# Linear attention and mixture-of-depths on one core: the early loads, one copy, one exponential and the warm-up rearranged

## Chip, cores and metric

One core of a Trainium2 chip runs the whole program. The metric is the device time of one execution in microseconds (us). Three runs of the kernel before took 196.46, 196.93 and 198.37 us; the median is 196.93 us.

## What is computed

The program is an attention block without a softmax over pairs, followed by a block that sends 128 of 576 rows of each batch through a small MLP. There are 8 batches, 8 heads, 576 rows and 64 columns per head.

```python
q_s = exp(q - max(q, -1));  q_s /= sum(q_s, -1)
k_s = exp(k - max(k, 2));   k_s /= sum(k_s, 2)
kv  = einsum('bhsd,bhse->bhde', k_s, v)
x   = einsum('bhsd,bhde->bhse', q_s, kv)     # regrouped to (8, 576, 512)
scores = x @ w_gate
out = x
for b: top = the 128 rows of b with the highest score
       xe = x[b, top]
       out[b, top] = xe + sigmoid(scores[b, top]) * (relu(xe @ w1) @ w2)
```

w1 is 512 x 1024 and w2 is 1024 x 512, all in float32.

## The kernel before

A *unit* is a batch and half of its heads, so there are 16 units u = 0 to 15, two per batch. The raw inputs of a unit are loaded into tiles `raw["q"]`, `raw["k"]`, `raw["v"]`; there are three of each (`LD = 3`), so the load of unit u + 3 waits until unit u is read. Every load is cut into two DMAs, all issued by SyncE's queue (SP) except one half of k(0), which ScalarE issues. A DMA that is issued takes the next of eight completion semaphores in turn, and waits for the DMA that had it eight issues earlier.

For one unit, ScalarE takes the exponential of k (`k_exp`, tile ke) and of q (`q_exp`, tile qe, two parts of 5 and 4 row groups). An engine copies v into a tile `v_ones` with columns of ones beside it (`v_copy`, or `v_copy_part` by half of the heads). TensorE (PE) multiplies ke with v_ones (`kv_mm`, or `kv_mm_parts` for unit 1), VectorE (DVE) normalizes that into `kv_w` (`kv_out`, `kv_out_part`), PE transposes qe (`q_t`), ScalarE or VectorE copies the result out of PSUM to qT, and PE multiplies qT with kv_w (`x_mm`). VectorE takes sums and scales (`x_sums`, `x_scale`), and SP stores the rows (`x_store`).

When both units of a batch are done, the scores are known (`score`). PE and ScalarE lay them out as a row (`score_row`, tile srow), and VectorE compares each row group with it (`compare`, line 443) to get a rank. For batch 0 alone, `select` (lines 498 to 512) turns the ranks into a 0/1 matrix and PE multiplies the rows with it, so that the chosen rows are gathered and transposed at once: five rounds of compare, one-hot matrix and matmuls. The other batches fetch their rows by an indirect DMA. The MLP runs on PE in pieces between the attention steps.

Nothing is scheduled by a planner here: `manual_schedule` keeps every engine to the order of the code, and lines 857 to 930 write out by hand the order of units 0 to 2, which is where the change lies. Before that, 12 matmuls on ones (line 173, `WARM = 12`) keep PE busy from the start. The lines that the change and the prediction speak of are: 220 to 223 (the memsets of the unused last row group of k(1), v(1), k(2), and the loads of unit 1 and of k(2)), 871 to 876 (the memset of v(2) by VectorE between the two halves of `q_t(0)`, then the loads of v(2), q(2) and of w1), 885 and 886 (v(1) copied half by VectorE and half by GpSimd), and 906 to 913 (score, `kv_mm(2)` in two halves around `score_row(0)`, and the exponentials of q(2)).

Of the kernel before, what the change touches and what calls it, by code (L numbers as in the profile page):

```python
# [17 lines left out]
def kernel(  # L18
# [23 lines left out]
    nc = tc.nc  # L42
    B, H, S, D = q.shape
    DM, F = moe_w1.shape
    P = 128
    R = 5
    N2 = R - 1
# [13 lines left out]
    NV = 5  # L61
    TURNED = frozenset((11, 13, 15))
    HC = 32
    WARM = 12
    assert S == 64 * T and D == 64 and DM == H * D and DM == 512 and H % 4 == 0
    assert 1 < capacity < S and KF == 8 and NQ == 2
    assert B * S <= 32 * 256
# [31 lines left out]
    def rows_of(b, upward):  # L99
# [12 lines left out]
    def load(u, which, queues=(nc.sync, nc.sync)):  # L112
        b, qd = units[u]
        for what in which:
            src = {"q": q, "k": k, "v": v}[what]
            t = raw[what][u % LD]
            first = src[place(b), 4 * qd].offset
            if what == "q" and u in by_vector:

                for g in range(4):  # L120
                    i, c = divmod(g, 2)
                    nc.sync.dma_start(
                        out=t.rearrange("p h r d -> p (h r d)")[HC * g:HC * (g + 1)],
                        in_=bass.AP(tensor=src.tensor, offset=first + 2 * i * SD + HC * c,
                                    ap=[[T * D, HC], [D, T], [SD // 2, 4], [1, HC]]))
                continue
            if what == "q":
                for h in range(2):
                    queues[h].dma_start(out=t[:, h].rearrange("p r d -> p (r d)"),
                                        in_=bass.AP(tensor=src.tensor, offset=first + 2 * h * SD,  # L130
                                                    ap=[[T * D, P], [1, T * D]]))
                continue
            for n, rows in ((1, N2), (0, R)):
                queues[n].dma_start(
                    out=t[n::2, :, :rows].rearrange("p h r d -> p h (r d)"),
                    in_=bass.AP(tensor=src.tensor, offset=first + n * R * D,
                                ap=[[T * D, 64], [SD, 4], [1, rows * D]]))

    ctx.enter_context(tc.manual_schedule())
    for what in "kv":  # L140
# [13 lines left out]
    def load_w1(half):  # L154

        c = slice(half * F // 2, (half + 1) * F // 2)
        for d in range(0, KD, 2):
            nc.sync.dma_start(out=w1[:, d:d + 2, c],
                              in_=moe_w1[d * P:(d + 2) * P, c].rearrange("(d p) f -> p d f", p=P))

    def load_w2(n):
        half = KF // 2
        nc.sync.dma_start(out=w2[:, n * half:(n + 1) * half],
                          in_=moe_w2[n * half * P:(n + 1) * half * P].rearrange("(f p) d -> p f d", p=P))

# [5 lines left out]
    ones_f = const.tile([1, D], F32, name="ones_f")  # L171
    nc.vector.memset(ones_f, 1.0)
    for n in range(WARM):
        nc.tensor.matmul(out=w_ps, lhsT=ones_b[:, :P], rhs=ones_b, start=True, stop=True)
# [42 lines left out]
    whole = const.tile([P, B * R], I32, name="whole")  # L217
    rest = const.tile([P, B * R], I32, name="rest")
    nc.gpsimd.iota(whole.rearrange("p (b r) -> p b r", b=B), pattern=[[S, B], [1, R]], base=0, channel_multiplier=T)
    for n, what in ((1, "k"), (1, "v"), (2, "k")):  # L220
        nc.gpsimd.memset(raw[what][n][:, :, N2], 0.0)
    load(1, "qkv")
    load(2, "k")
    vals = const.tile([P, B, R, NV], BF16, name="vals")
    valid_r = const.tile([P, 3, R], F32, name="valid_r")
    s_all = const.tile([P, B, R], F32, name="s_all")
# [548 lines left out]
        nc.vector.tensor_sub(t, t, qm.to_broadcast([P, 2 * T, D]))  # L775

    def general():
        nonlocal by_vector
        by_vector = frozenset()
        for half in range(2):  # L780
            load_w1(half)
            load_w2(half)
        for b in range(B):
            for u in (NQ * b, NQ * b + 1):
                load(u, "kvq")
                shift(u)
# [82 lines left out]
    fill(3)  # L869

    q_t(0, 0, on_vector=True)
    nc.vector.memset(raw["v"][2][:, :, N2], 0.0)
    q_t(0, 1)
    load(2, "vq")
    load_w1(0)
    load_w1(1)
    q_exp(1, 0)
    q_exp(1, 1)
    k_exp(1)
# [2 lines left out]
    x_mm(0, 1)  # L882
    x_sums(0, (0,))
    x_scale(0, 0)
    v_copy_part(1, 0, nc.vector)
    v_copy_part(1, 1, nc.gpsimd)
    x_sums(0, (1,))
    x_scale(0, 1)
# [15 lines left out]
    x_mm(1, 1)  # L904
    x_sums(1, (1,))
    score(0)
    kv_mm(2, (0,))
    score_row(0, tag="mm")
    kv_mm(2, (1,))
    q_exp(2, 0)  # L910
    q_exp(2, 1)
    x_scale(1, 0)
    x_scale(1, 1)
# [292 lines left out]
```

## Time and profile before

| | |
|---|---|
| median of three runs | 196.93 us |
| the profiled execution's own time | 197.7 us |
| its span, from the first to the last instruction | 195.8 us |
| granted TensorE clock | 0.993 |
| PE busy, share of the span | 184.2 us, 94% |
| VectorE, ScalarE, GpSimd busy | 130.4, 99.7, 72.7 us |
| DMA | 46.67 MB, mean 238 GB/s over the span |

A page of the profile describes one execution. A row of the timeline begins with the start of a group of instructions in us from the span's start and the time that the group took, then come the engine, the line, the operation, what it writes and reads, how many there were, and in brackets the idle time of the engine before it with what ended it. PEld is PE's loading of weights, which runs beside its matmuls; SPq is SyncE's queue, whose rows are the issues of DMAs. `<-issue` means that the engine waited for nothing that the profile shows. A float32 matmul of the program appears as two matmuls and two weight loads in the rows, so `x40` of line 311 are 20 in the code.

### The profile page before, as it was taken

Reading aid. Unit: us, or ns where it says so; the run is one execution under the profiler, and the core shown is the slowest. Engines: PE = TensorE matmul, PEld = TensorE weight load, DVE = VectorE, ACT = ScalarE, POOL = GpSimd, SP = SyncE. Lnnn points to the kernel's source line nnn. Section 1 sums busy time; section 2 is a strip of 40 time slices with the busy share of each in tenths; the row PEclk is TensorE's granted clock in tenths of the full one; section 3 lists DMA queues with packets and bytes.
Section 4 is the critical chain, followed back from the end, with each engine's and each line's share of the span. In section 5 each row is a group of like instructions: output and inputs, shape, how many; then the busy total and the mean of one; then the engine's idle time right before and its main releaser. Section 6 shows DMA issues by size and latency. Waiting matters only on the chain.

```text
span 195.8 us, 7049 instructions
## 1 busy us (share of the span) xinstructions
PE 184.2 (94%) x2927; PEld 156.0 (80%) x2927; DVE 130.4 (67%) x429; ACT 99.7 (51%) x160; POOL 72.7 (37%) x131
## 2 busy tenths in 40 slices
PE   5798899999999999999999999999999999999990
PEld 2466699894679996769999888899998889898860
DVE  6377966494669749928978989489959955444010
ACT  3474625658199759938675759365423133312100
POOL 8013551100860392099682312242314354701230
PEclk9999999999999999999999999999999999999997
DMA  5999999999999999989999799989451514010011
GB/s 153 364 365 378 378 368 364 328 388 352 341 379 374 336 314 363 308 248 152 312 325 320 130 317 330 273 160 257 158 121 57 121 38 149 32 54 5 3 56 63
DMA packets 48361, 46.67 MB, mean 238 GB/s; under 512 B 16321, under 2 KB 41921, under 8 KB 48322
## 3 DMA queue, kind: packets, MB, share of 16 engines
q1 hardware_dynamic: 46768, 41.62, 67.4%
q0 software_dynamic: 1280, 4.20, 6.7%
q8 instruction: 25, 0.41, 0.9%
q10 hardware_dynamic: 274, 0.33, 0.5%
q14 instruction: 14, 0.11, 0.2%
HBM read 34.61 MB, written 11.53 MB: 236 GB/s over the span
## 4 chain that ended last, share of the span: by engine, by line
PE 85%; DVE 6%; DMA 3%; issue 1%; ACT 1%; POOL 1%; POOLq 0%; DVEq 0%
PE mm L704 19%; PE mm L648 18%; PE tp L311 10%; PE x L375 10%; PE mm L555 8%; PE mm L564 8%; PE x L347 4%; DMA v<-in_v_dram 3%; PE mm L509 2%; PE tp L432 2%; PE x L530 2%; DVE xs L393 1%; DVE v_ones L280 0%; PE tp L468 0%; DVE v_ones L275 0%
## 5 line engine op out<-in xcount | busy, mean ns | idle before, releaser
L443 DVE SCALAR_TENSOR_TENSOR junk<-srow,s,stairs 128x576 bf16<-128x576 f32 x40 | 33.4, 834 | 1.5 <-ACT srow L435 0.8
L393 DVE TENSOR_TENSOR xs<-x,qrec 128x640 f32<-128x640 f32 x32 | 25.2, 815 | 0.0
L375 PE MATMUL x<-kv_w,qT 64*64 64x66 f32 x1152 | 23.2, 222 | 1.2 <-issue 0.5
L375 PEld LDWEIGHTS x<-kv_w,qT 64*64 64x64 f32 x1152 | 20.7, 134 | 4.5 <-issue 2.1
L352 ACT COPY qT<-x 128x512 f32<-128x512 f32 (+1 forms) x24 | 14.3, 643 | 17.1 <-PE x L347 16.6
L311 PE MATMUL tp<-v_ones,ke 128*64 128x65 f32 x600 | 21.6, 224 | 1.4 <-DVE v_ones L275 1.1
L704 PE MATMUL mm<-w,hT 128*128 128x256 f32 x96 | 22.2, 379 | 0.0
L249 ACT ACTIVATE ke<-k 128x1280 f32<-128x1280 f32 x16 | 20.4, 1274 | 3.4 <-issue 1.4
L311 PEld LDWEIGHTS tp<-v_ones,ke 128*64 128x64 f32 x600 | 19.2, 137 | 3.6 <-issue 1.9
L493 POOL DMA_INDIRECT xr<-out_dram,idx x8 | 8.1, 1018 | 36.3 <-DVE no L486 9.8
L704 PEld LDWEIGHTS mm<-w,hT 128*128 128x128 f32 x96 | 17.8, 190 | 2.2
L257 ACT ACTIVATE qe<-q 128x640 f32<-128x640 f32 (+1 forms) x26 | 16.4, 683 | 5.7 <-DMA q<-in_q_dram 3.0
L704 PE MATMUL mm<-tw,hT 128*128 128x256 f32 (+1 forms) x80 | 17.6, 363 | 0.0
L648 PE MATMUL mm<-xT,w 128*128 128x128 f32 x144 | 17.5, 276 | 0.0
L275 ACT COPY v_ones<-v 128x1280 f32<-128x1280 f32 x12 | 15.1, 1258 | 3.8 <-PE tp L311 2.5
L648 PEld LDWEIGHTS mm<-xT,w 128*128 128x128 f32 x144 | 16.8, 192 | 0.1
L555 PE MATMUL mm<-xT,w 128*128 128x128 f32 x128 | 16.7, 281 | 0.0
L713 POOL TENSOR_TENSOR o<-o,xr 128x256 f32<-128x256 f32 x9 | 6.8, 757 | 23.6 <-ACT o L712 23.6
L564 PE MATMUL mm<-w,hT 128*128 128x512 f32 x32 | 15.6, 611 | 0.0
L555 PEld LDWEIGHTS mm<-xT,w 128*128 128x128 f32 x128 | 15.0, 191 | 0.5
L704 PEld LDWEIGHTS mm<-tw,hT 128*128 128x128 f32 x80 | 13.8, 190 | 2.0 <-DVE o L717 0.4
L386 DVE RECIPROCAL qrec<-x 128x10 f32<-128x10 f32 x32 | 7.0, 217 | 12.6 <-PE x L375 12.2
(162 smaller groups left out, 311.2 us busy)
## 6 DMA issues: line engine op xcount, KB each, us to landing
q<-in_q_dram SPq DMA_DIRECT2D x26, 288.0 KB, 5.7
v<-in_v_dram SPq DMA_DIRECT2D x16, 320.0 KB, 5.4
out_dram<-xs SPq DMA_DIRECT2D x16, 320.0 KB, 5.6
k<-in_k_dram SPq DMA_DIRECT2D x15, 320.0 KB
k<-in_k_dram SPq DMA_DIRECT2D x16, 256.0 KB, 5.9
v<-in_v_dram SPq DMA_DIRECT2D x16, 256.0 KB
out_dram<-xs SPq DMA_DIRECT2D x16, 256.0 KB, 4.8
w<-in_moe_w_dram SPq DMA_DIRECT2D x4, 512.0 KB, 8.2
```

What stands on the lines that cost most here:

```text
L249: nc.scalar.activation(out=ke, in_=raw["k"][u % LD], func=AF.Exp)
L257: nc.scalar.activation(out=st["qe", u][:, r0:r1], in_=qr[:, r0:r1], func=AF.Exp)
L275: copy(out=v_ones[:, :, :, :D], in_=raw["v"][u % LD])
L311: nc.tensor.matmul(out=kv[part(h), i], lhsT=ke[:, 2 * h + i, r], rhs=vo[:, 2 * h + i, r], start=(r == 0), stop=(r == N2))
L352: nc.scalar.copy(out=to, in_=src)
L375: nc.tensor.matmul(out=to[:, r * C:(r + 1) * C], lhsT=lhsT, rhs=kw[part(i), a], start=True, stop=True)
L393: nc.vector.tensor_mul(xs[b][:, :, qd, :, a].rearrange("p r i d -> p i r d"), x[:, :, :, :D], rec.to_broadcast([P, 2, R, D]))
L443: nc.vector.scalar_tensor_tensor(junk, st["srow", b], st["s", b][:, r:r + 1], not_before[r], op0=OP.subtract, op1=OP.is_ge, accum_out=st[" ...
L555: nc.tensor.matmul(out=h_ps[:, f % HT * m:(f % HT + 1) * m], lhsT=w1[:, d, f * P:(f + 1) * P], rhs=xT[:, d, :m], start=(d == 0), stop=(d = ...
L564: nc.tensor.matmul(out=st["y", b][:m], lhsT=st["hT", b][:, f // HT, f % HT, :m], rhs=w2[:, f], start=(f == 0), stop=(f == KF - 1))
L648: nc.tensor.matmul(out=out_ps[:, f * m:(f + 1) * m], lhsT=w[:, k, f * P:(f + 1) * P], rhs=x()[:, k], start=first and f == 0 and k == 0, st ...
L704: nc.tensor.matmul(out=ps_of[to][:m, c:c + step], lhsT=st["hT", a][:, n, f, :m], rhs=w[:, f, c:c + step], start=first and f == 0, stop=f = ...
```

## The change

Five things are done. VectorE's half of the copy of v(1) is given to GpSimd, which then does both halves. The memset of v(2) goes from VectorE to GpSimd, into the loop of line 220, and the loads of v(2), q(2) and w1 are written directly behind that of k(2), so that none of them waits for VectorE any more. The exponential of the first part of q(2) stands ahead of the score row in ScalarE's order. Every load of q, k, v, w1 and w2 is given a wait for the load that was issued six loads earlier. The warm-up is 22 matmuls of 280 columns in place of 12 of 512.

```diff
-    WARM = 12
+    WARM = 22
+    AHEAD = 6
+    transfers = []
+
+    def paced(inst):
+        ins = inst.ins
+        if transfers is not None:
+            transfers.append(ins.name)
+            if len(transfers) > AHEAD:
+                tc.add_manual_dep(ins, transfers[-1 - AHEAD], mybir.DependencyInfo(
+                    mybir.DependencyClass.Sync, mybir.DependencyReason.DATA))
...
-                    queues[h].dma_start(out=t[:, h].rearrange("p r d -> p (r d)"),
+                    paced(queues[h].dma_start(out=t[:, h].rearrange("p r d -> p (r d)"),
...
-        nc.tensor.matmul(out=w_ps, lhsT=ones_b[:, :P], rhs=ones_b, start=True, stop=True)
+        nc.tensor.matmul(out=w_ps[:, :280], lhsT=ones_b[:, :P], rhs=ones_b[:, :280], start=True, stop=True)
...
-    for n, what in ((1, "k"), (1, "v"), (2, "k")):
+    for n, what in ((1, "k"), (1, "v"), (2, "k"), (2, "v")):
         nc.gpsimd.memset(raw[what][n][:, :, N2], 0.0)
     load(1, "qkv")
-    load(2, "k")
+    load(2, "kvq")
+    load_w1(0)
+    load_w1(1)
...
     q_t(0, 0, on_vector=True)
-    nc.vector.memset(raw["v"][2][:, :, N2], 0.0)
     q_t(0, 1)
-    load(2, "vq")
-    load_w1(0)
-    load_w1(1)
...
-    v_copy_part(1, 0, nc.vector)
+    v_copy_part(1, 0, nc.gpsimd)
     v_copy_part(1, 1, nc.gpsimd)
...
     score(0)
+    q_exp(2, 0)
     kv_mm(2, (0,))
     score_row(0, tag="mm")
     kv_mm(2, (1,))
-    q_exp(2, 0)
     q_exp(2, 1)
```

`paced` is put around the other loads in the same way. In the branch for inputs out of range (`general`), which these inputs do not take, it is switched off.

ScalarE around the score row of batch 0, before (q_78 is q(2), k_81 is k(2), srow the row of scores):

```order
L249 ACTIVATE ke<-k_81 128x1280
L435 ACTIVATE srow<-tp 128x512
L435 ACTIVATE srow<-mm 128x64
L257 ACTIVATE qe<-q_78 128x640
L257 ACTIVATE qe<-q_78 128x512
L352 COPY qT<-x 128x5x2x64
```

ScalarE there, now:

```order
L263 ACTIVATE ke<-k_81 128x1280
L271 ACTIVATE qe<-q_78 128x640
L449 ACTIVATE srow<-tp 128x512
L449 ACTIVATE srow<-mm 128x64
L271 ACTIVATE qe<-q_78 128x512
L366 COPY qT<-x 128x5x2x64
```

The first part's exponential has gone ahead of both pieces of the score row; the second part stays behind them.

SP's queue at the loads of unit 2, with the waits of each, before (v_84 is v(2), w_97 is w1; DMAHW0 to DMAHW7 are the eight completion semaphores):

```order
L134 DMA k_81<-in_k_dram 64x4x256 [waits DMAHW5_49]
L134 DMA k_81<-in_k_dram 64x4x320 [waits DMAHW6_49,Pool_49]
L134 DMA v_84<-in_v_dram 64x4x256 [waits DMAHW7_49]
L134 DMA v_84<-in_v_dram 64x4x320 [waits DMAHW0_49,DVE_49]
L129 DMA q_78<-in_q_dram 128x576 [waits DMAHW1_49]
L129 DMA q_78<-in_q_dram 128x576 [waits DMAHW2_49]
L158 DMA w_97<-in_moe_w_dram 128x2x512 [waits DMAHW3_49]
```

SP's queue there, now:

```order
L146 DMA k_81<-in_k_dram 64x4x256 [waits DMAHW7_49]
L146 DMA k_81<-in_k_dram 64x4x320 [waits DMAHW0_49,Pool_49]
L146 DMA v_84<-in_v_dram 64x4x256 [waits DMAHW1_49]
L146 DMA v_84<-in_v_dram 64x4x320 [waits DMAHW2_49,Pool_49]
L141 DMA q_78<-in_q_dram 128x576 [waits DMAHW3_49]
L141 DMA q_78<-in_q_dram 128x576 [waits DMAHW4_49]
L170 DMA w_97<-in_moe_w_dram 128x2x512 [waits DMAHW5_49]
```

The order of the loads is the same; the wait for VectorE is gone, and each load waits for a semaphore that is two DMAs younger than before.

GpSimd from its last memsets to its first work on the scores, before (v_83 is v(1)):

```order
L219 IOTA whole 128x40
L221 MEMSET k_80 128x4x64
L221 MEMSET v_83 128x4x64
L221 MEMSET k_81 128x4x64
L280 COPY v_ones<-v_83 128x2x5x64
L280 COPY v_ones<-v_84 128x2x5x64 x2
```

GpSimd there, now:

```order
L231 IOTA whole 128x40
L233 MEMSET k_80 128x4x64
L233 MEMSET v_83 128x4x64
L233 MEMSET k_81 128x4x64
L233 MEMSET v_84 128x4x64
L294 COPY v_ones<-v_83 128x2x5x64 x2
L294 COPY v_ones<-v_84 128x2x5x64 x2
```

One memset and one copy have come over from VectorE.

More of the change, by code (lines that the diff above doesn't have):

```diff
@@ L121, in load @@
                     i, c = divmod(g, 2)
-                    nc.sync.dma_start(
+                    paced(nc.sync.dma_start(
                         out=t.rearrange("p h r d -> p (h r d)")[HC * g:HC * (g + 1)],
                         in_=bass.AP(tensor=src.tensor, offset=first + 2 * i * SD + HC * c,
-                                    ap=[[T * D, HC], [D, T], [SD // 2, 4], [1, HC]]))
+                                    ap=[[T * D, HC], [D, T], [SD // 2, 4], [1, HC]])))
                 continue
@@ L128, in load @@
                 for h in range(2):
-                    queues[h].dma_start(out=t[:, h].rearrange("p r d -> p (r d)"),
-                                        in_=bass.AP(tensor=src.tensor, offset=first + 2 * h * SD,
-                                                    ap=[[T * D, P], [1, T * D]]))
+                    paced(queues[h].dma_start(out=t[:, h].rearrange("p r d -> p (r d)"),
+                                              in_=bass.AP(tensor=src.tensor, offset=first + 2 * h * SD,
+                                                          ap=[[T * D, P], [1, T * D]])))
                 continue
             for n, rows in ((1, N2), (0, R)):
-                queues[n].dma_start(
+                paced(queues[n].dma_start(
                     out=t[n::2, :, :rows].rearrange("p h r d -> p h (r d)"),
                     in_=bass.AP(tensor=src.tensor, offset=first + n * R * D,
-                                ap=[[T * D, 64], [SD, 4], [1, rows * D]]))
+                                ap=[[T * D, 64], [SD, 4], [1, rows * D]])))
     ctx.enter_context(tc.manual_schedule())
@@ L157, in load_w1 @@
         for d in range(0, KD, 2):
-            nc.sync.dma_start(out=w1[:, d:d + 2, c],
-                              in_=moe_w1[d * P:(d + 2) * P, c].rearrange("(d p) f -> p d f", p=P))
+            paced(nc.sync.dma_start(out=w1[:, d:d + 2, c],
+                                    in_=moe_w1[d * P:(d + 2) * P, c].rearrange("(d p) f -> p d f", p=P)))
     def load_w2(n):
         half = KF // 2
-        nc.sync.dma_start(out=w2[:, n * half:(n + 1) * half],
-                          in_=moe_w2[n * half * P:(n + 1) * half * P].rearrange("(f p) d -> p f d", p=P))
+        paced(nc.sync.dma_start(out=w2[:, n * half:(n + 1) * half],
+                                in_=moe_w2[n * half * P:(n + 1) * half * P].rearrange("(f p) d -> p f d", p=P)))
     ones_b = const.tile([P, 4 * P], BF16, name="ones_b")
@@ L777, in general @@
     def general():
-        nonlocal by_vector
+        nonlocal by_vector, transfers
         by_vector = frozenset()
+        transfers = None
         for half in range(2):
```

## The prediction

> **What bounds the kernel now.** I first ask in which stretch PE, busy for 94% of the span, is idle at all. The windows view gives the busy time and the count of each engine in three stretches.
>
> ```profile
> core 0: us, PE busy (x) PEld busy (x) DVE busy (x) ACT busy (x) POOL busy (x), PEclk, DMA share, GB/s
> 0.00:28.00 28.00, 22.69 (x383) 16.44 (x387) 19.62 (x79) 12.47 (x18) 11.02 (x30) 1.00 0.96 333
> 28.00:100.00 72.00, 71.63 (x1455) 58.65 (x1456) 50.07 (x179) 50.09 (x77) 30.98 (x51) 1.00 1.00 326
> 100.00:190.00 90.00, 89.40 (x1095) 80.93 (x1094) 60.70 (x173) 37.11 (x66) 30.13 (x51) 1.00 0.54 151
> ```
>
> From 28 us on PE bounds: it lacks 0.37 us in 72 and 0.60 in 90. Before that it is idle for 5.31 us, of which 2.07 pass before its first matmul. All that the change touches lies in these 28 us, and a gain there is kept if PE reaches its dense part sooner. So the question is when select's matmuls end. The timeline shows PE's rows up to there.
>
> ```profile
> 16.70 0.46 PE L375 MATMUL x<-kv_w,qT 64*64 64x66 f32 x15 [0.23 <-DVE krec L286]
> 17.38 0.51 PE L375 MATMUL x<-kv_w,qT 64*64 64x66 f32 x18 [0.23 <-issue]
> 18.25 0.33 PE L375 MATMUL x<-kv_w,qT 64*64 64x66 f32 x5
> 18.80 0.80 PE L311 MATMUL tp<-v_ones,ke 128*64 128x65 f32 x20 [0.21 <-POOL v_ones L280]
> 19.53 0.65 PE L432 MATMUL tp<-ident,s_all 128*128 128x128 f32 x4
> 20.22 0.80 PE L311 MATMUL tp<-v_ones,ke 128*64 128x65 f32 x20
> 21.61 0.77 PE L340 MATMUL x<-ident,qe 128*128 128x128 f32 x5 [0.58 <-ACT qe L257]
> 22.30 0.46 PE L347 MATMUL x<-ident,qe 64*128 64x64 f32 x8
> 22.69 0.94 PE L509 MATMUL mm<-hT,xs 128*128 128x128 f32 x6
> 24.02 3.95 PE L509 MATMUL mm<-hT,xs 128*128 128x128 f32 x34 [0.39 <-issue]
> ```
>
> Four waits stand there: 0.21 us for GpSimd's copy of v(2), 0.58 for the exponential of q(2), and two that end on nothing visible, 0.23 and 0.39. Select ends at 24.02 + 3.95 = 27.97 us.
>
> **The copy of v(1).** These rows of the timeline are the copy and its users.
>
> ```profile
> 13.88 0.72 POOL L280 COPY v_ones<-v 128x640 f32<-128x640 f32 x1 [9.06 <-DMA v<-in_v_dram]
> 13.97 0.97 DVE L280 COPY v_ones<-v 128x640 f32<-128x640 f32 x1
> 14.20 0.74 PE L340 MATMUL x<-ident,qe 128*128 128x128 f32 x5
> 15.09 1.39 PE L299 MATMUL tp<-v_ones,ke 128*64 128x65 f32 x40 [0.15 <-DVE qrec L386]
> 15.19 0.81 DVE L393 TENSOR_TENSOR xs<-x,qrec 128x640 f32<-128x640 f32 x1
> 18.02 1.39 POOL L280 COPY v_ones<-v 128x640 f32<-128x640 f32 x2 [3.43 <-PE x L375]
> ```
>
> Now GpSimd does one half from 13.88 to 14.60 and the other to about 15.3; PE needs them at 14.94 (when its transposes end) and some 0.7 us later. So `kv_mm_parts(1)` starts at 14.94 instead of 15.09 and VectorE loses 0.97 us of work: 0.15 us for PE. But the next stop gives it back: `kv_mm(2)` waits until 18.80 for GpSimd's copy of v(2), which began at 18.02. **Worth 0**, as long as v(2) comes when it did.
>
> **The loads unbound.** Does it come sooner? The first row is SP's wait for the memset, the next the issue of v(2), then what the loads of v take from issue to landing, then the DMA engines in three windows.
>
> ```profile
> SPq L134 <- DVE v L872: 1.8, 1, 1.8
> 9.65 3.23 SPq L134 DMA_DIRECT2D v<-in_v_dram x2
> DMA to landing us min/median/max: 5.1/5.4/6.1
> 12.00:14.00 2.00, 1.97 (x81) 1.77 (x81) 1.32 (x5) 2.00 (x3) 0.12 (x1) 1.00 1.08 365
> 14.00:16.00 2.00, 1.84 (x38) 1.48 (x38) 1.97 (x6) 1.55 (x3) 0.59 (x1) 1.00 1.08 362
> 16.00:18.00 2.00, 1.55 (x72) 1.30 (x71) 1.07 (x9) 1.27 (x1) 0.00 (x0) 1.00 1.05 380
> ```
>
> The second half of v(2) was the last issue of a row that ends at 9.65 + 3.23 = 12.88, so it went out at about 12.3; 5.4 more is 17.7, which is when GpSimd could start. The DMA engines are full throughout (share 1.05 to 1.08): a load of 288 KB takes 0.81 us at 365 GB/s, so eight of them are 6.5 us of queue, and SP's wait of 1.8 never emptied it. Issued sooner, v(2) stands longer in the same queue. Worth between 0 and 0.34 us (0.15 and 0.21 of the two waits above); I take **0**, since the windows show no hole. The memset (0.27 us on VectorE) goes to GpSimd at about 4.8 us, where it has nothing to do until 13.88.
>
> **Six ahead.** Six loads are 4.9 us of queue, and the wait is for the landing of the load six places ahead, so five, some 4 us, still stand before it when SP issues. That covers the way from issue to the first bytes, which the trace bounds only from above, by 5.1 us with the queue full. I take **0**. Ends: each load late by the two that are missing, 1.6 us, or the waits of others shortened (rivals). Behind a waiting load on SP stand the later loads and then, from unit 0's store on, the stores.
>
> **The exponential.** ScalarE's and VectorE's rows behind the score row, and the issue and landing of the loads of q:
>
> ```profile
> 13.58 0.43 SPq L129 DMA_DIRECT2D q<-in_q_dram x1
> q<-in_q_dram SPq DMA_DIRECT2D x26, 288.0 KB, 5.7
> 20.22 0.60 ACT L435 ACTIVATE srow<-tp 128x512 f32<-128x512 f32 x1 [2.31 <-PE tp L432]
> 20.82 1.26 ACT L257 ACTIVATE qe<-q 128x640 f32<-128x640 f32 x2
> 21.04 0.82 DVE L443 SCALAR_TENSOR_TENSOR junk<-srow,s,stairs 128x576 bf16<-128x576 f32 x1 [0.27 <-ACT srow L435]
> 26.15 0.29 DVE L504 TENSOR_TENSOR hT<-slot_no,rank 128x128 f32<-128x128 f32 x1
> ```
>
> q(2) lands at about 13.58 + 5.7 = 19.3. ScalarE is idle for 2.31 us before 20.22, so one exponential (1.26 / 2 = 0.63) runs from 19.4 to 20.0 and the score row keeps its start. The other ends at 20.93 + 0.63 = 21.5. PE transposes q(2) from 21.02 on, as soon as `kv_mm(2)` ends: 0.58 us sooner. What is late next is VectorE: its five rounds start with the score row at 21.04 as before, and the last one-hot matrix is there at 26.15 + 0.29 = 26.44. PE's last eight matmuls take 8 x 3.95 / 34 = 0.93, so select ends at 27.4 to 27.5. **Gain 0.50**, if nothing else holds PE.
>
> **Instruction blocks.** Something else does. The first row counts what PE ran between the two unexplained waits; the others are the queue that carries instructions, and the next such wait.
>
> ```profile
> 17.37:24.01 6.64, 5.45 (x125) 4.62 (x126) 5.35 (x15) 3.57 (x7) 4.20 (x11) 1.00 1.05 382
> q8 instruction: 25, 0.41, 0.9%
> 36.56 0.58 PE L375 MATMUL x<-kv_w,qT 64*64 64x66 f32 x25 [0.25 <-issue]
> ```
>
> 125 + 126 = 251 instructions and a few waits lie between, and q8 moved 25 packets of 0.41 MB / 25 = 16.4 KB. I read this as PE taking its program in blocks of that length, and waiting twice for one that was late: 6.64 us from one to the next, while the DMA engines are full. [...]
>
> The ten added warm-up matmuls are 20 instructions, so each later boundary falls ten matmuls earlier: behind the fifth matmul of `x_mm(1)` instead of the fifteenth, and in the middle of the eight of line 347 instead of behind select's sixth. After the second boundary there is 4 x 0.05 + 6 x 0.116 = 0.9 us more to do than before, hence select ends at that block's arrival + 0.9 + 3.95. If the arrival stays at 24.02 this is 28.87, 0.9 later than now; if it is ahead of 22.6, the 0.50 is kept whole. The first block is asked for earlier too, by between 0.2 us (ten weight loads of 0.60 / 33, first row below) and 0.7 (if the request goes ahead of PE's wait of 0.65 for qT, same row). While the second is under way, the six-ahead rule holds back the last of w1's four loads.
>
> ```profile
> 12.03 0.60 PEld L375 LDWEIGHTS x<-kv_w,qT 64*64 64x64 f32 x33 [0.65 <-DVE qT L350]
> 2.07 4.45 PE L174 MATMUL tp<-ones_b 128*128 128x512 bf16 x12 [2.07 <-DVE second_p L182]
> 8.51 1.39 PE L311 MATMUL tp<-v_ones,ke 128*64 128x65 f32 x40 [1.09 <-DVE v_ones L275]
> ```
>
> I take 0.7 and 0.3 for the two, 1.0 off the arrival, 23.0: select ends at 27.85, so the blocks **take back 0.38** of the 0.50. The wait of 0.25 at 36.56 I let go, since the later blocks are asked for sooner as well: **gain 0.25**, between 0 and 0.25.
>
> **Warm-up.** 22 x 280 = 6160 columns stand for 12 x 512 = 6144, so its 4.45 us hardly change, and behind it PE waits 1.09 us for v(0) anyway: 0. If every added matmul cost 0.1 us, this 1.0 us would still fit into that wait.
>
> **Sum.** -0.50 + 0.38 - 0.25 = -0.37 us. The profiled execution took 197.7 us, 1.9 outside its span, and lies 0.8 above the median of the runs shown; I subtract from the median: 196.93 - 0.37 = **196.6 us**.
>
> **Rivals.** (1) *The blocks decide.* The second block comes no earlier than 23.9, select ends 0.8 us later than now, and with the 0.25 kept or not the time is 197.5 to 197.8: not faster. For it: the interval of 6.64 us is shown, and PE asks for the block 2 us before 23.9. Against it: the first request must then gain almost nothing. It decides from an arrival at 23.1 on. (2) *Six ahead shortens the blocks' way.* If fewer queued loads let a block through 1 us sooner, the waits of 0.23, 0.39 and 0.25 go, the 0.50 stays whole, and some later idle time (0.37 + 0.60 in the windows) with it: -1.5 to -2.0, so 195.2. For it: the waits lie where the DMA share is above 1. Against it: even six loads keep the engines full. (3) *Six ahead starves the queue.* Loads land up to 1.6 us later. The row below is the next such user; PE takes its result at 32.65, so 1.1 us are free after the exponentials' end at 31.51.
>
> ```profile
> 30.25 1.26 ACT L257 ACTIVATE qe<-q 128x640 f32<-128x640 f32 x2 [0.49 <-DMA q<-in_q_dram]
> 32.65 0.78 PE L347 MATMUL x<-ident,qe 64*128 64x64 f32 x18
> ```
>
> That is 0.5 us at unit 3 and, if it returns at three or four more units, 1.5 to 2: 198.4 to 198.9. Against it: the five loads in between.
>
> **Numbers.** Forecast (196.1 to 197.0) 0.52, rival 1 0.25, rival 2 0.15, rival 3 0.08. The range 195.2 to 197.8 takes in the first two and most of rival 2; outside lie rival 3 and the end of rival 2. A measurement tells about 1%, 2 us, from no change, and only the far ends of rivals 2 and 3 reach that: faster 0.08, the same 0.88, slower 0.04.
>
> **What would show it.** Right: line 340's wait of 0.58 gone and q(2)'s transposes at 21.0 to 21.1; `kv_mm(2)` still starting near 18.8 after GpSimd's copy; the score row still at 20.2; a wait on "issue" in the middle of the eight matmuls of line 347, ended at 22.8 to 23.3; select over at 27.6 to 28.1; DMA share above 1 to 30 us. Wrong: `kv_mm(2)` before 18.5 (the loads did come sooner), no wait on "issue" before 24 us, a row of PE or ScalarE that waits for a load after 32 us, or a difference that arises after 40 us.

## The result and the profile after

The change is slower. Its median over six executions is 200.62 us (199.01 to 202.83), that of the kernel before 197.32 us beside it; the ratio is 1.0138, with an interval of 1.0091 to 1.0185. Measured twice more on other chips it is 1.0105 (1.0042 to 1.0167) and 1.0152 (1.0082 to 1.0222). Executions of one kernel differ by some 4 us here, and the ratios leave out those more than 1.5% above the fastest of their kernel. The profiled execution is the slowest of the six: 202.83 us with a span of 201.0 us, 5.2 us more than the span before. So its rows show where time can be lost, and the ratios how much of it is lost as a rule.

The windows view of the change, in the stretches of the prediction:

```profile
core 0: us, PE busy (x) PEld busy (x) DVE busy (x) ACT busy (x) POOL busy (x), PEclk, DMA share, GB/s
0.00:28.00 28.00, 22.84 (x374) 17.53 (x374) 16.88 (x69) 12.58 (x18) 10.83 (x30) 0.94 0.89 301
28.00:100.00 72.00, 69.14 (x1319) 55.76 (x1318) 46.22 (x168) 47.43 (x73) 31.48 (x48) 0.98 0.98 314
100.00:190.00 90.00, 89.56 (x1217) 81.88 (x1216) 64.67 (x189) 40.11 (x71) 32.22 (x54) 1.00 0.59 168
```

The DMA engines moved 301 GB/s up to 28 us, where it was 333. PE lacks 2.86 us between 28 and 100 us, where it lacked 0.37: there is a loss long after select. And in two stretches the granted clock is below 1.

First the early stretch. The change's timeline, PE's rows to the end of select (line 523 is the old 509, 354 the old 340):

```profile
15.76 1.47 PE L313 MATMUL tp<-v_ones,ke 128*64 128x65 f32 x40 [0.78 <-POOL v_ones L294]
...
20.43 1.27 PE L325 MATMUL tp<-v_ones,ke 128*64 128x65 f32 x20 [1.35 <-POOL v_ones L294]
21.63 1.12 PE L446 MATMUL tp<-ident,s_all 128*128 128x128 f32 x4
...
24.11 0.76 PE L354 MATMUL x<-ident,qe 128*128 128x128 f32 x5
24.80 0.46 PE L361 MATMUL x<-ident,qe 64*128 64x64 f32 x8
25.19 5.02 PE L523 MATMUL mm<-hT,xs 128*128 128x128 f32 x40
30.14 0.73 PE L389 MATMUL x<-kv_w,qT 64*64 64x66 f32 x33
```

The rows to set beside those of before are 15.09 (now 15.76), 18.80 (20.43) and 21.61 (24.11). The exponential's wait of 0.58 us is gone, as forecast, but what replaced it is larger: 0.78 and 1.35 us of waiting for copies of v, whose loads came late: GpSimd starts its copy of v(2) at 19.65 us, released by the load, where it started at 18.02. There is no wait on "issue" in these rows; PE came to the middle of the eight matmuls of line 361 only at about 25.0 us, later than the block came in most of the runs below (a "block" is the author's reading of PE's waits on "issue"; no view shows what PE waits for there). Select ends at 25.19 + 5.02 = 30.2 us instead of 28.0. The four matmuls of line 446 take 1.12 us where line 432 took 0.65; the next view has a granted clock of 0.64 there, where it was 1.00. The windows view of the change, 2 us each after the first row (the column ahead of the last two is the granted clock):

```profile
10.00:20.00 10.00, 7.79 (x224) 5.93 (x222) 6.21 (x27) 5.71 (x8) 1.73 (x3) 1.00 0.95 315
20.00:22.00 2.00, 1.57 (x22) 1.45 (x23) 1.26 (x2) 0.74 (x1) 1.78 (x7) 0.64 0.82 275
22.00:24.00 2.00, 2.00 (x25) 1.67 (x23) 0.41 (x1) 1.22 (x3) 0.56 (x3) 0.51 0.93 300
74.00:76.00 2.00, 1.04 (x10) 0.79 (x8) 1.82 (x5) 0.71 (x2) 2.00 (x2) 1.00 1.04 364
76.00:78.00 2.00, 0.14 (x2) 0.17 (x3) 1.08 (x3) 0.00 (x0) 1.78 (x6) 1.00 1.03 366
78.00:80.00 2.00, 2.00 (x13) 2.00 (x13) 1.93 (x5) 1.48 (x2) 1.85 (x3) 0.65 0.96 340
80.00:82.00 2.00, 2.00 (x3) 0.79 (x3) 1.93 (x5) 2.00 (x4) 0.35 (x1) 0.50 1.06 363
```

After both of PE's longest waits here (1.35 and 2.82 us) the granted clock falls to 0.5 for some 3 us. Each pair of rows, 0.64 and 0.51, then 0.65 and 0.50, is followed by 1.00. By an estimate from some 3 us at a clock of 0.5, some 1.5 us of work are lost behind each wait itself.

Second the loss at 75 us. The timeline of the kernel before has three rows there that the prediction did not show: VectorE scales the rows of unit 5, SP issues their stores, and GpSimd fetches the chosen rows of batch 2 (units 4 and 5), which reads what the stores wrote.

```profile
56.36 1.54 DVE L393 TENSOR_TENSOR xs<-x,qrec 128x640 f32<-128x640 f32 x2
...
59.16 1.31 SPq L404 DMA_DIRECT2D out_dram<-xs  x2
...
66.93 1.00 POOL L493 DMA_INDIRECT xr<-out_dram,idx  x1 [8.70 <-DVE krec L319]
...
73.77 0.63 PE L530 MATMUL x<-ident,xr 128*128 128x128 f32 x4
```

The same four in the timeline of the change:

```profile
57.72 1.55 DVE L407 TENSOR_TENSOR xs<-x,qrec 128x640 f32<-128x640 f32 x2
...
63.18 1.31 SPq L418 DMA_DIRECT2D out_dram<-xs  x2
...
70.45 1.00 POOL L507 DMA_INDIRECT xr<-out_dram,idx  x1 [10.00 <-DMA out_dram<-xs]
...
77.86 0.63 PE L544 MATMUL x<-ident,xr 128*128 128x128 f32 x4 [2.82 <-DVE junk L457]
```

The rows are ready 1.4 us later (59.27 against 57.90), their stores are issued 4.0 us later, the fetch now waits for the store, and PE waits 2.82 us for the fetch. (The releaser that stands there, junk, is only what came last on the record; GpSimd's row names the store.) PE's transposes start 4.1 us later than before. The store stands on SP behind the loads of units 7 and 8, each with its six-ahead wait. Other profiles of the change follow below.

### The profile page after: what moved, and what is told of

It is laid out like the page before. It is cut to its first block, busy times and chain, and to the rows that moved or that the text cites. A ratio compares the mean times of both kernels' runs of the same rounds, so it can differ in the third digit from the quotient of the medians.

```text
span 201.0 us, 7070 instructions
## 1 busy us (share of the span) xinstructions
PE 187.4 (93%) x2937; PEld 159.5 (79%) x2937; DVE 129.2 (64%) x427; ACT 100.1 (50%) x160; POOL 76.7 (38%) x133
## 4 chain that ended last, share of the span: by engine, by line
PE 74%; DMA 11%; DVE 6%; POOL 4%; issue 1%; ACT 1%; POOLq 0%; SPq 0%; DVEq 0%
PE mm L718 18%; PE mm L662 18%; PE mm L578 8%; PE tp L325 8%; PE x L389 7%; DMA v<-in_v_dram 6%; PE mm L569 5%; PE x L361 3%; DMA out_dram<-xs 3%; PE mm L523 2%; DMA k<-in_k_dram 2%; PE tp L446 2%; DVE junk L457 2%; PE x L544 2%; POOL sw L626 1%; POOL tw L626 1%
## 5 line engine op out<-in xcount | busy, mean ns | idle before, releaser
L325 PEld LDWEIGHTS tp<-v_ones,ke 128*64 128x64 f32 x600 | 19.7, 142 | 3.9 <-POOL v_ones L294 1.5
L662 PE MATMUL mm<-xT,w 128*128 128x128 f32 x144 | 17.5, 276 | 0.0
L569 PE MATMUL mm<-xT,w 128*128 128x128 f32 x128 | 17.3, 288 | 0.0
L662 PEld LDWEIGHTS mm<-xT,w 128*128 128x128 f32 x144 | 16.8, 192 | 0.1
L578 PE MATMUL mm<-w,hT 128*128 128x512 f32 x32 | 16.7, 648 | 0.0
L569 PEld LDWEIGHTS mm<-xT,w 128*128 128x128 f32 x128 | 15.6, 197 | 0.5
```

Source lines behind the costliest of these rows:

```text
L325: nc.tensor.matmul(out=kv[part(h), i], lhsT=ke[:, 2 * h + i, r], rhs=vo[:, 2 * h + i, r], start=(r == 0), stop=(r == N2))
L569: nc.tensor.matmul(out=h_ps[:, f % HT * m:(f % HT + 1) * m], lhsT=w1[:, d, f * P:(f + 1) * P], rhs=xT[:, d, :m], start=(d == 0), stop=(d = ...
L578: nc.tensor.matmul(out=st["y", b][:m], lhsT=st["hT", b][:, f // HT, f % HT, :m], rhs=w2[:, f], start=(f == 0), stop=(f == KF - 1))
L662: nc.tensor.matmul(out=out_ps[:, f * m:(f + 1) * m], lhsT=w[:, k, f * P:(f + 1) * P], rhs=x()[:, k], start=first and f == 0 and k == 0, st ...
```

## The experiments

S is the theory that the six-ahead wait starves the DMA queue or holds up SP; B that the moved instruction blocks cost; G that GpSimd's copy or the exponential does. Each ratio is to the kernel before on the same chip. All in one table, with the medians:

| run | what it is | ratio (95%) | median, us: this, before |
|---|---|---|---|
| e1 | change without the six-ahead wait | 1.0009 (0.9973 to 1.0045) | 199.10, 198.67 |
| e3 | change, wait for the seventh ahead | 1.0027 (0.9988 to 1.0066) | 199.44, 198.67 |
| e4 | change, wait for the fourth ahead | 1.0879 (1.0797 to 1.0961) | 215.48, 198.67 |
| e2 | before, six-ahead wait alone | 1.0009 (0.9967 to 1.0051) | 200.42, 198.67 |
| e7 | before, new warm-up alone | 0.9996 (0.9957 to 1.0034) | 198.55, 198.72 |
| e8 | before, exponential moved alone | 1.0003 (0.9964 to 1.0043) | 198.25, 198.72 |
| e12 | before, GpSimd's copy and loads unbound alone | 1.0024 (0.9984 to 1.0064) | 198.75, 198.15 |
| e5 | change without six ahead, old warm-up | 1.0035 (0.9993 to 1.0078) | 199.51, 198.72 |
| e6 | change with the old warm-up | 1.0008 (0.9960 to 1.0056) | 199.45, 198.72 |
| e9 | the change again | 1.0105 (1.0042 to 1.0167) | 201.19, 198.15 |
| e10 | change, six ahead on the first loads only | 1.0024 (0.9987 to 1.0061) | 198.59, 198.15 |
| e11 | change, six ahead from unit 3 on only | 1.0112 (1.0047 to 1.0177) | 200.25, 198.15 |
| e13 | change, units 7 and 8 without the rule | 1.0012 (0.9910 to 1.0114) | 200.56, 201.20 |
| e14 | change, the rule at units 7 and 8 only | 1.0037 (0.9955 to 1.0119) | 199.51, 201.20 |
| e15 | change, unit 5's stores by GpSimd | 1.0095 (1.0012 to 1.0178) | 200.98, 201.20 |
| e16 | before, unit 5's stores by GpSimd | 1.0035 (0.9945 to 1.0125) | 199.92, 201.20 |
| e17 | e13 again | 1.0107 (1.0044 to 1.0169) | 200.80, 198.24 |
| e18 | the change a third time | 1.0152 (1.0082 to 1.0222) | 200.98, 198.24 |

### How many loads ahead (e1 to e4)

The edit is the number alone; 99 makes the rule empty. e2 puts `paced` with 6 into the kernel before and changes nothing else.

```diff
-    AHEAD = 6
+    AHEAD = 99        # e1;  7 in e3, 4 in e4
```

e1: 

> The changed kernel without the wait for the sixth load ahead (the other four edits stay). Theory S (the six-ahead wait starves the DMA queue between 10 and 30 us, so v(1), k(2), v(2), q(2) land 1 to 2 us later): the time falls back to before or under it, ratio to before 0.994 to 1.002; v(2) is copied by GpSimd from about 18.0 again, DMA rate in 10 to 20 us back at 370 GB/s from 315. Rival G (GpSimd's two copies, the exponential ahead of the score row, or the warm-up cost the time): it stays 1.2 to 1.5% above before. Rival B (the instruction blocks cost it): it stays at 0.5 to 1% above, with a wait on issue near 23 to 24 us.

e2: 

> The kernel before with the six-ahead wait alone. Theory S: slower by most of the 1.4%, ratio 1.008 to 1.018, v(2) copied from about 19 to 19.7 us and DMA rate in 10 to 20 us near 315 GB/s. Rivals G and B: ratio within 0.3% of 1.000, DMA rate near 370 GB/s.

e3: 

> The changed kernel with a wait for the seventh load ahead in place of the sixth. Theory S: a smaller loss, ratio 0.996 to 1.008, since one more load (0.81 us of queue) covers most of the 3.4 to 3.9 us from issue to first landing; rate in 10 to 20 us 345 to 370 GB/s. Rivals G and B: as the change, 1.010 to 1.018.

e4: 

> The changed kernel with a wait for the fourth load ahead. Theory S: much slower, since at most four loads are under way in a round trip of about 4.5 to 5 us, that is 240 to 265 GB/s in place of 370 over the first 30 us: 6 to 10 us more than before, ratio 1.03 to 1.05. Rivals G and B: no more than the change, 1.010 to 1.018.

The windows view, 10 to 20 us: of e4, then of e3, then of e1.

```profile
10.00:20.00 10.00, 7.07 (x201) 5.89 (x204) 4.76 (x21) 5.47 (x8) 1.38 (x2) 0.92 0.91 261
```

```profile
10.00:20.00 10.00, 8.95 (x268) 7.49 (x266) 6.56 (x27) 7.14 (x10) 3.19 (x7) 1.00 1.04 359
```

```profile
10.00:20.00 10.00, 9.02 (x261) 7.40 (x258) 6.65 (x28) 6.81 (x10) 3.28 (x7) 1.00 1.07 375
...
26.00:28.00 2.00, 2.00 (x11) 2.00 (x11) 1.10 (x9) 0.00 (x0) 0.47 (x2) 0.50 1.09 384
```

Four loads ahead give 261 GB/s, six 315 to 354 (all nine profiles with the rule on the first loads), seven 359, and the kernels without it 363 to 375. The time follows: 8.8% more with four (twice what was expected), 0.3% with seven and 0.1% without the rule. So the change loses its time only with the rule in it. An estimate from rows of the prediction agrees for six: a load takes 0.81 us of the full queue and lands 5.4 us after its issue, so 5.4 / 0.81 = 6.7 loads are under way on average in the kernel before; six are 0.90 of that, or 329 of 365 GB/s. For four it gives 218, which is too low, because with fewer loads in the line each lands sooner: of the loads of the first 22 us, those of k whose landing the trace has take 4.2 us in e4 and 6.3 in the kernel before, those of q 3.7 and 5.2. The 6.7 is therefore no threshold. In the order of SP's queue, `[waits DMAHW5_49]` shows that the kernel before already had such a rule by its eight semaphores: eight DMAs ahead. The change took it from eight to six.

e1 shows another wait, which the first profile of the change did not have. Its PE rows in the timeline:

```profile
23.73 0.34 PE L361 MATMUL x<-ident,qe 64*128 64x64 f32 x4 [1.83 <-issue]
24.00 6.36 PE L523 MATMUL mm<-hT,xs 128*128 128x128 f32 x40
```

With the loads in time again, the block is late in the middle of the eight, where the prediction had put it: 1.83 us. After it the clock is 0.50 (the row of 26 to 28 us above), and select takes 6.36 us. So the exponential's gain is not kept even without the rule. Select ends at 30.4 us here and in e3, as late as in the first profile of the change. The spans of these two profiles are 198.0 and 196.9 us (195.8 before, 201.0 in the result), and the ratios are 1.0009 and 1.0027: so late a select does not alone make the loss.

e2 alone is not clear. Its ratio is 1.0009, but its median lies 0.9% above: six of its twelve executions took more than 200.5 us, of the kernel before beside it five of 29. Its profiled execution, one of the six, has the same wait at 75 us (timeline):

```profile
76.07 0.73 PE L542 MATMUL x<-ident,xr 128*128 128x128 f32 x4 [2.12 <-DMA xr<-out_dram,idx]
```

### Warm-up, exponential, copy (e5 to e8, e12)

```diff
-    WARM = 22
+    WARM = 12         # and the matmuls 512 wide: e5 (without six ahead) and e6 (with it)
```

e5: 

> The change without the six-ahead wait and with the old warm-up, 12 matmuls of 512 columns: the instruction blocks begin at the same matmuls as in the kernel before. Theory B (in the version without the six-ahead wait the moved block boundary stalls PE by 1.83 us in the middle of q(2)'s second part, at 23.7 us, and the idle time lowers the granted clock in select): the wait for a block is back behind select's sixth matmul, 0.2 to 0.5 us long, the clock of 20 to 30 us is 0.95 or more, select takes 4.9 us or less and ends at 27.2 to 28.0 us (30.3 with 22 warm-up matmuls); ratio to the kernel before 0.992 to 0.999. Rival G (GpSimd's copy or the exponential's new place cost the time, the blocks only show it): q(2)'s second part still waits, select ends at 29 us or later; ratio 1.000 to 1.005.

e6: 

> The whole change but for the warm-up, which stays 12 matmuls of 512 columns. Theory S (the six-ahead wait alone starves the queue, the loads of unit 2 land late whatever the warm-up): DMA rate of 10 to 20 us 310 to 345 GB/s, v(2) lands after 18.5 us, select ends at 29.0 to 30.2 us, ratio to the kernel before 1.008 to 1.016, as with 22 warm-up matmuls. Theory B alone (the block decides in the whole change too): select ends at 28.0 or sooner and the ratio falls to 1.003 or less.

e7: 

> The kernel before with the warm-up of 22 matmuls of 280 columns and nothing else. Theory B: the wait for an instruction block moves from behind select's sixth matmul to the middle of the eight of q(2)'s second part, 0.9 us before that place's old time, and is 0.8 to 1.8 us long, the granted clock of the next window falls below 0.95, select ends at 28.8 to 30.3 us (27.97 before); ratio 1.003 to 1.010. Rival (the block comes as much sooner as it is asked for sooner): wait 0.2 to 0.5, select ends at 27.9 to 28.2, ratio 0.998 to 1.002.

e8: 

> The kernel before with the exponential of q(2)'s first part ahead of the score row and nothing else. Prediction's term: the wait of 0.58 us of q(2)'s transposes goes, select's block still comes at 24.0, so PE reaches it 0.5 sooner and waits 0.9 there: select ends at 27.9, 0 gained; ratio 0.998 to 1.000. Theory B's second half (a longer idle time of PE lowers the granted clock afterwards): the wait of 0.9 is followed by a clock below 0.97 and select ends at 28.2 to 29; ratio 1.001 to 1.005. If the block comes sooner with PE being sooner: select ends at 27.5, ratio 0.996 to 0.998.

e12: 

> The kernel before with v(1) copied by GpSimd and the loads of unit 2 and w1 unbound from VectorE, and nothing else (old warm-up, exponential in its old place, no six-ahead wait). Prediction's terms: 0 for both, select ends at 27.6 to 28.0 us, ratio 0.998 to 1.000. Rival G (GpSimd's two halves in a row delay kv of unit 1 or its later work): kv of unit 1 starts after 15.5 us, ratio 1.001 to 1.004, as in the version without six ahead and with the old warm-up (1.0035).

Theory B's forecast for e5 failed: the wait behind select's sixth matmul is back, but it is 0.77 us and another of 1.51 us stands at the block before it (20.56 us in its timeline), select ends at 31.0, and the time is no better than e1's. About 2 us of that lateness were there before either wait (`x_mm(0)` starts at 14.14 us, where it started at 12.03 before): PE is busy for 0.96 us of the two from 8 to 10, and the granted clock is 0.80, 0.50 and 0.85 in the three windows of 2 us from 8 us on. e6 failed theory S as it stood: with the rule and the old warm-up the ratio is 1.0008, though its profile has 327 GB/s, a wait of 2.46 us for the rows of batch 2 at 77.7 us, and a median 0.4% up. Alone, no part reaches 0.3% by its ratio; the intervals reach 0.6%.

The timeline of e7, then that of e8:

```profile
23.66 0.34 PE L347 MATMUL x<-ident,qe 64*128 64x64 f32 x4 [1.12 <-issue]
23.93 4.73 PE L509 MATMUL mm<-hT,xs 128*128 128x128 f32 x40
...
75.43 0.63 PE L530 MATMUL x<-ident,xr 128*128 128x128 f32 x4 [1.02 <-DMA xr<-out_dram,idx]
```

```profile
20.91 0.77 PE L340 MATMUL x<-ident,qe 128*128 128x128 f32 x5
...
23.79 3.95 PE L509 MATMUL mm<-hT,xs 128*128 128x128 f32 x34 [0.65 <-issue]
```

e7: the boundary moved as predicted, and the block came at 23.66 instead of 24.02: 0.36 us sooner, where the prediction took 0.7 without the six-ahead rule and 1.0 with it. PE waits 1.12 us, the clock stays at 1.00, and select takes 4.73 us at it. It ends 0.7 us later than before, but the ratio is 0.9996, so theory B's loss of 0.3 to 1% did not come. The third row shows 1.02 us of waiting for the rows of batch 2 without any six-ahead rule: the fetch goes out at 67.56 us, released by VectorE, and PE starts on the rows 7.9 us later, where they landed after 6.2 us before. e8: PE comes 0.7 us earlier to q(2) and gets 0.23 of it behind the block, at 23.79 instead of 24.02. e12: kv of unit 1 starts at 14.96 without any wait, so GpSimd's two halves cost nothing when v(1) is in time; the wait of 0.78 in the change was for the load. But select does not end at 27.6 to 28.0 us as expected. The timeline of e12:

```profile
18.77 0.51 PE L389 MATMUL x<-kv_w,qT 64*64 64x66 f32 x18 [1.74 <-issue]
...
24.86 4.96 PE L523 MATMUL mm<-hT,xs 128*128 128x128 f32 x40
```

The block that cost 0.23 us at 17.38 in the kernel before is 1.74 us late here, at the same fifteenth matmul of `x_mm(1)`, the granted clock is 0.50 from 20 to 22 us, and select ends at 29.8. No part of e12 moves that boundary, so the old place has long waits in some executions too (1.51 us in e5, 0.67 in e2).

### Where the rule costs (e9 to e11)

e9 is the change again. e10 and e11 switch the rule off after the loads of w1, or on only there:

```diff
-    load_w1(1)
+    load_w1(1); transfers = None      # e10;  e11 starts with None and puts [] here
```

e9: 

> The change once more as it is, beside the three below, since the comparison of the result rests on six executions and single parts so far gave 0.9996 to 1.0035. Theory S+B (the parts are harmless or nearly so alone, and add up only together): 1.006 to 1.016 again, select ends at 29.5 to 30.3 us, PE idle for 2 us or more between 74 and 79 us. Rival C (the loss of the result is in good part scatter between executions): 1.000 to 1.005.

e10: 

> The change with the six-ahead wait for the first loads alone (units 0 to 2 and w1); from unit 3 on no such wait. Theory S early (the first loads cost the time, by way of select): select ends at 29.5 to 30.3 us, no wait of PE at 75 us, ratio 1.006 to 1.012. Theory S late (the later loads cost it: they hold back the stores behind them on SP's queue, and with them the fetch of batch 1's rows): PE's idle time between 74 and 79 us is gone, ratio 1.000 to 1.004.

e11: 

> The change with the six-ahead wait from unit 3 on alone; the first loads (units 0 to 2 and w1) go without. Theory S early: v(2) lands at 17.7 us, the instruction block waits in the middle of q(2)'s second part as without any such wait, ratio 1.000 to 1.004. Theory S late: the same there, and then PE idle for 2 to 3 us between 74 and 79 us, ratio 1.008 to 1.016.

The rows that PE waits for are those of batch 2; the expectations called them batch 1's. e11's timeline, and behind it what SP waited for between 48 and 52 us:

```profile
51.15 1.37 SPq L146 DMA_DIRECT2D k<-in_k_dram  x2
...
56.36 1.54 DVE L407 TENSOR_TENSOR xs<-x,qrec 128x640 f32<-128x640 f32 x2
...
62.09 1.31 SPq L418 DMA_DIRECT2D out_dram<-xs  x2
...
70.09 1.00 POOL L507 DMA_INDIRECT xr<-out_dram,idx  x1 [9.88 <-DMA out_dram<-xs]
...
76.21 0.63 PE L544 MATMUL x<-ident,xr 128*128 128x128 f32 x4 [1.92 <-DMA xr<-out_dram,idx]
```

```profile
SPq L146 <- DMA k<-in_k_dram: 1.6, 1, 1.6
```

This is the clearest of all: SP stands for 1.6 us on the landing of an earlier load of k, where the kernel before has no such wait in these 4 us. The rows of unit 5 are ready at 57.90 us, to the hundredth as before, and the stores go out at 62.09 instead of 59.16, behind k(7), which went out at 51.15 (48.44 before), and the loads that follow it. The fetch is 3.2 us late and PE waits 1.92 us. The later loads alone cost 1.1%, the first loads alone (e10) 0.2%, with 0.6% at the end of the interval. e10's profile itself says little of the fetch, since PE is 3.5 us late there after a wait of 2.34 us for the block and a select that ends at 32.5.

e9's timeline, and behind it a row of its windows:

```profile
23.13 0.34 PE L361 MATMUL x<-ident,qe 64*128 64x64 f32 x4 [0.69 <-issue]
23.40 4.73 PE L523 MATMUL mm<-hT,xs 128*128 128x128 f32 x40
...
75.70 0.94 PE L544 MATMUL x<-ident,xr 128*128 128x128 f32 x4 [1.95 <-DMA xr<-out_dram,idx]
```

```profile
76.00:78.00 2.00, 2.00 (x12) 2.00 (x11) 1.93 (x5) 1.32 (x2) 1.85 (x3) 0.50 1.01 339
```

In this execution select went nearly as predicted, though `kv_mm(2)` waited 0.90 us for GpSimd's copy: the block came at 23.13 (predicted 23.0), and select ended at 23.40 + 4.73 = 28.1 (27.85). The time was lost at 75 us all the same, and the wait was followed by a granted clock of 0.50, as the row of 76 to 78 us shows.

### Units 7 and 8, and the store (e13 to e18)

```diff
-            if len(transfers) > AHEAD:
+            if len(transfers) > AHEAD and unit[0] not in (7, 8):   # e13, e17;  "in" for e14
...
-        x_store(s)
+        x_store(s, nc.gpsimd if s == 5 else nc.sync)               # e15; e16 in the kernel before
```

e13: 

> The change without the six-ahead wait at the loads of units 7 and 8; all other loads keep it. Theory U7 (k and v of unit 7 wait, everything behind them on SP's queue is 2 to 3 us late, unit 5's store among it, and the fetch of batch 2's rows waits for that store): unit 5's store is issued within 2.3 us of xs being done (3.9 to 4.2 in the change), GpSimd's fetch is released by VectorE again, no wait of PE above 1 us between 74 and 79 us, ratio 1.000 to 1.005. Rival (the loads of units 3 to 5 carry it): the wait at 75 us stays, ratio 1.007 to 1.014.

e14: 

> The change with the six-ahead wait at the loads of units 7 and 8 alone. Theory U7: DMA rate of 10 to 20 us as without the rule (370 to 376 GB/s), SP idle between q(6) and k(7) for 1 to 2 us, unit 5's store issued 3.5 to 4.5 us after xs is done, PE idle for 1.5 to 3 us between 74 and 79 us, ratio 1.006 to 1.013. Rival (units 3 to 5): no such wait, ratio 1.000 to 1.004.

e15: 

> The change as it is, but unit 5's two stores are issued by GpSimd, which has nothing to do there, and so stand behind no load. Theory store (the late loads cost only by the store behind them): the fetch is released by VectorE, the wait of PE at 75 us is below 1 us, ratio 1.000 to 1.005 although every load waits as before. Rival (the loads themselves or the lower DMA rate cost it): a wait of PE for a load's user appears instead or the one at 75 us stays, ratio 1.007 to 1.014.

e16: 

> The kernel before with unit 5's stores issued by GpSimd. In its profiled execution the fetched rows had landed 0.6 us before PE took them. If other executions of the kernel before lose time there, as the spread of its runs by 2 percent may mean: ratio 0.993 to 0.998, and fewer runs above 200 us. If not: 0.998 to 1.002.

e17: 

> The change without the six-ahead wait at the loads of units 7 and 8, once more. Units 7 and 8 carry the loss: no wait of PE above 1 us between 70 and 79 us, ratio 0.998 to 1.004, and 0.006 or more below the change beside it. Rival (the loads of units 3 to 5 or the early ones carry it): ratio 1.007 or more, as the change.

e18: 

> The change as it is, a third time, as the measure for the run beside it: 1.008 to 1.015, with PE idle for 1.5 to 3 us between 70 and 79 us. If the loss of the result was the scatter of a chip: below 1.005.

In e15 the fetch no longer waits for a store, and PE takes its rows at 75.0 us without waiting. But the timeline shows the wait elsewhere:

```profile
70.42 1.39 PE L325 MATMUL tp<-v_ones,ke 128*64 128x65 f32 x40 [1.60 <-ACT v_ones L289]
```

With the store out of the way, unit 7's load of v is late (issued at 52.33 us, 49.81 in the kernel before), with ScalarE's copy of it, as the rival of e15 had it. The time does not settle it: the ratio is 1.0095, the median is below that of the kernel before beside it, and the executions of that chip scatter widely. e14 failed theory U7: with the rule at units 7 and 8 alone k(7) goes out at 48.55 us, GpSimd's fetch is released by VectorE at 67.7, and no wait arises at 75. k(7) is hardly late there (48.44 us before), and SP's row of v(7) takes 1.92 us where it took 1.35. So the rule at unit 7 seems to bite only when the loads of units 3 to 6 ahead of it are late too; one profile each stands for this. e13 and e17 are one kernel. In e13's profile the loss at 75 us is gone (span 195.8 us), though k(7) goes out at 50.22 and the store 3.2 us after its rows are ready, not within 2.3 us; the interval of its ratio, 0.9910 to 1.0114, tells nothing. e17 is 1.0107, which is the rival's number and only 0.0045 below e18 beside it, and its profile has the loss in another place. Its timeline and its windows:

```profile
24.56 0.48 PE L361 MATMUL x<-ident,qe 64*128 64x64 f32 x4 [2.60 <-issue]
24.97 7.37 PE L523 MATMUL mm<-hT,xs 128*128 128x128 f32 x40
```

```profile
26.00:28.00 2.00, 2.00 (x11) 2.00 (x11) 1.15 (x9) 0.00 (x0) 0.52 (x2) 0.50 0.87 262
28.00:30.00 2.00, 2.00 (x11) 2.00 (x11) 0.00 (x0) 0.00 (x0) 0.23 (x1) 0.50 0.86 256
```

A block that comes 2.60 us late and then a granted clock of 0.50 from 24 to 30 us: select takes 7.37 us instead of 4.73 and ends at 32.3. e18, the change itself, has a wait of 2.10 at 26.03, select over at 32.7 and then, against its expectation, no wait at 75 us: PE is 4.1 us late there, and the fetch, released by VectorE, is in time. It was late from the first matmuls on, as a row of its timeline shows:

```profile
9.38 2.42 PE L325 MATMUL tp<-v_ones,ke 128*64 128x65 f32 x40 [1.70 <-DVE v_ones L289]
```

It waits 1.70 us for v(0); the 40 matmuls then take 2.42 us where they took 1.39 before, the granted clock of 10 to 20 us is 0.86, and `x_mm(0)` starts at 14.47 us where it started at 12.03 before. The losses at the two places replace each other in part: in the three of the change select ends 2.2, 0.2 and 4.7 us later than in the kernel before, PE waits 2.82, 1.95 and 0 us for the rows of batch 2, and the transposes of these rows start 4.1, 1.9 and 4.1 us late. Of the six profiles with the six-ahead rule on all loads from unit 3 on and the store on SP, five wait 1.92 to 2.82 us for these rows (the result, e2, e6, e9, e11; not e18). Of the eight without the rule on these loads (the kernel before, e1, e5, e7, e8, e10, e12, e16) only e7 does, for 1.02 us, though PE is itself 1.6 to 3.5 us late there in e1, e5 and e10. e16 shows no gain in the kernel before (1.0035, 0.9945 to 1.0125); nothing that was run is faster than it beyond the measurement's uncertainty.

## Why the prediction was wrong, point by point

**The step that failed is "Six ahead".** The prediction set five queued loads, "some 4 us", against the way from issue to the first bytes, and took 0. That way was known only to be below 5.1 us, so the row did not carry the 0; and what SP waits for is a load's landing (2.8 us in all up to 14 us in the first profile of the change, for landings of k and v; 0.4 us for landings in the kernel before), for which the same row said 5.4 us. The runs show that the five loads did not cover it: 315 to 354 GB/s with the rule where the others have 363 to 375, and 1.1% more time from the rule on the later loads alone (e11). The far end that the step named, each load 1.6 us late, is what GpSimd's copy of v(2) shows in the first profile (19.65 instead of 18.02). Its rival 3 had the mechanism, with 0.08 for it and a size of 1.5 to 2 us against 2 to 3 measured (1.05 to 1.5% of 198). What it had not followed is the sentence of its own that the stores stand behind the waiting loads: it looked for late users among the exponentials, and the user at which PE lost most was the fetch behind the stores of unit 5, which the prediction never priced.

**What bounds the kernel** was read too narrowly. "All that the change touches lies in these 28 us" is not so: the rule is on every load, and the prediction's own fences showed PE without idle time up to 100 us, which tells that later waits just fit, not by how much. Its list of what would prove it wrong did name a difference that arises after 40 us. The fetch had landed 0.6 us before PE took it (issue at 66.93, 6.2 us to landing, taken at 73.77).

**Instruction blocks**: place and direction right. e11 and e14 have the first wait behind the fifth matmul of `x_mm(1)` (0.20 us to 17.38, 0.45 to 17.29), and the wait in the middle of the eight was there in e1, e3, e7, e9, e10, e11, e14, e17 and e18. In the profile of the result there is none, and in e13 and e15 the eight take 0.75 and 0.78 us instead of 0.46, which leaves room for 0.3. The arrival was mis-sized. Taken at 23.0, it was 23.1 in e9, but 23.7 to 23.9 in e1, e3, e7, e11 and e14, and 24.6 to 26.0 in e17, e10 and e18, and in e10 and e18 PE was 2.4 us late already at `x_mm(0)`: rival 1 (from 23.1 on) decides in most of them, where it was a quarter of the chances. When a block is asked for, no view shows, so the 1.0 taken off its arrival was an estimate that no run shows; in its place the wait in the eight ended 0.36 us before 24.02 in e7, without the six-ahead rule, and 0.89 in e9, with it. One such wait is up to 2.60 us long (e17).

**The exponential**: -0.50 in the sum. Its own wait went, but e8 shows 0.23 us at the block and none in the time. That the block would take most of the gain back was forecast (0.38 of 0.50); in the change it took all of it, since even in e9 select ends 0.2 us later than before.

**The copy, the loads unbound, the warm-up's own time**: 0, and the ratios of e12 (1.0024) and e7 (0.9996) show nothing else, with intervals of 0.4% to either side. The gain of 0.25 us at 36.56 was too small for any run to show.

**The clock** was in no step. A wait of PE was priced at its length, but after most waits of 1.7 us and longer (e1, e2, e3, e9, e10, e12, e17, e18), and in the profile of the result, the granted clock is 0.50 to 0.53 in the lowest window of 2 us, and by an estimate from the windows 0.5 for about 3 us or more. In e1 that makes select 6.36 us long instead of 4.73, 1.6 us on top of a wait of 1.83.

**What stays open.** The late loads' rule costs 1.1% together with the new warm-up (e11), and both e2 and e6, which have the rule with the old warm-up, have ratios of 1.0009 and 1.0008 (up to 0.5 and 0.6% in the intervals) while their profiles show the same wait. So the rule costs its 1% as measured only beside the new warm-up, and why the warm-up should matter for that is not shown. How much of each wait at 75 us is the fetch's own, which landed after 6.2 us in the kernel before and 7.3 in the result, is not separated either. Nor is it settled which units' loads must wait for unit 7 to be late. The part of the block's wait in e17 and e18 that comes from the rule was not tried apart.

## What to carry to other kernels

A limit on transfers under way is first set beside the time until a transfer has landed, divided by the time that one takes of a full queue. Here that was 6.7, and the rate was 372 GB/s with eight, 359 with seven and 315 to 354 with six; the two limits near that number lowered the rate. Then follow everything that stands behind the waiting instruction on its queue to its last user, stores and the fetches behind stores first, however far down the program. A profile in which an engine is never idle does not tell how much margin the transfers behind it have; here it was 0.6 us. And the same change showed its loss in another place from one execution to the next: take several profiles before a cause is named.

## What the runs showed of the hardware

The granted clock often goes to about 0.50 after short waits of PE (0.50 to 0.52 in the lowest window of 2 us of the four that follow). With 1.83, 1.95, 2.10 and 2.60 us idle it fell (e1, e9, e18, e17), with 1.12, 1.27 and 1.43 it stayed at 1.00 (e7, e14, e11). No single length divides them: it fell after 1.35 us in the change, with 0.78 us idle 5 us earlier; it stayed after 1.60 in e15, 1.92 in e11 and 2.46 in e6. And from 8 to 10 us PE is busy for 0.96 us in e5 and 0.99 in e1, with a clock of 0.50 from 10 to 12 us in e5 and of 1.00 from 10 to 20 in e1.

One and the same program has its instruction block at 23.1 us in one execution and at 26.0 in another (e9 and e18). Most of that is PE's own lateness: `x_mm(1)`, in which the boundary before lies, starts at 16.64 and 18.93 us, so that the block comes 6.5 and 7.1 us behind it. Over the runs that show the wait this way is 6.5 to 7.7 us (the longest in e17), beside DMA engines with a share of 1.01 to 1.07 (18 to 24 us of e9, 18 to 26 of e18).
